# Channel mixing of the first batch spread over two attention batches, and four weight tiles converted ahead instead of twelve

## The chip, the cores and the metric

One core of a Trainium2 chip runs the whole program. The metric is the device time of one execution in microseconds (us). The engines named below are TensorE (PE, with its weight loads as PEld), VectorE (DVE), ScalarE (ACT), GpSimd (POOL) and SyncE (SP), whose queue issues nearly all DMAs.

## The reference

Three blocks follow each other on 4 batches of 448 tokens and 768 features, all in float32:

```python
attn_out = attn(q, k, v)                 # 12 heads of 64, causal mask, softmax
xt = x.transpose(0, 2, 1)                # x: attn_out as (batch, seq, 768)
h = relu(xt @ w_tok1) @ w_tok2           # token mixing, 448 -> 256 -> 448
u = x + h.transpose(0, 2, 1)
x = u + relu(u @ w_ch1) @ w_ch2          # channel mixing, 768 -> 1536 -> 768
theta = x @ w_theta
y = w_tok_r @ (x * cos(theta)) + w_tok_i @ (x * sin(theta))
u = x + y
out = u + relu(u @ w_ch)
```

The weights arrive as 64-bit floats. The chip rounds them to float32 and splits them into a high and a low part.

## The kernel before

**Attention.** Two heads make a pair, six pairs a batch, so there are 24 pairs. A pair has seven score tiles, and each tile is a *step*: 168 steps, 42 for a batch. `scores` (L252) does for one step the score matmul (L270), mask and row maximum on DVE (L277), the exponential on ACT (L279) and the transposition of the result. In pairs 0 to 11 PE transposes (L286) and ACT copies out (L288). From pair 12 (step 84) on, ACT and DVE split the result into two 16-bit halves (L107, L299) and a DMA transposes it (`pt<-ph`, L302), with three `ph` buffers. `pv` multiplies by the values four steps later, `finish` scales, and after every second pair `tokmix` does the token mixing for two 128-feature tiles of `u`. It also split each `u` tile into high and low parts (`ut`, nine buffers).

**Channel mixing** is cut into 96 *units*, 24 for a batch: 6 of `ch1_unit`, 6 of `ch2_unit`, and the same again for the second half of the 1536 features. A unit is 18 matmuls of 448 columns (L166 to L168, six tiles by three products) with one weight tile `ws` of 768 KB, and one evacuation on DVE (L387 or L395).

**Weights.** Each of the 24 channel weight tiles is converted once. ACT reads the raw data (L123), DVE does four bit operations (L130 to L134), ACT and DVE split it (L107, L114) into a `ws` tile (four buffers), and SP stores that to `w_c` (L433) for the later batches, which load it again (`ws<-w_c`, L161). `ROUND_STEPS` says at which step each conversion is written. Tiles below `EARLY` are converted ahead, stored, and loaded again when the first batch needs them. Tiles from `EARLY` on go from the conversion straight into their unit.

**Order.** Attention is written step by step with a priority of 500 instructions (`AHEAD`). Units and conversions are written between the steps without it, and a scheduler places them where it finds room, so they stand some steps behind the place where they are written. Once built, every engine and the SP queue run their own list strictly in its order. In the kernel before, unit number d*24//42 is written d steps after step 46: 24 units for each 42 steps.

**After attention** the remaining units run with the conversion of `w_theta` and `w_tok`, then the third block.

Of the kernel before, what the change touches and what calls it, by code (L numbers as in the profile page):

```python
# [19 lines left out]
B, H, S, D = 4, 12, 448, 64  # L20
E = H * D
NPR = H // 2
DT = E // P
# [5 lines left out]
BUFS = dict(ut=9, h2=6, acc=12, ws=4, wf=2, raw=2, sb=3, ph=3, pt=5)  # L29
NATIVE = {0, 1, 2, 3, 4, 5, 6, 7}  # L30
NATPV = {0, 1, 2, 3, 4, 5, 6, 7, 8, 9, 10, 11}
AHEAD, LAG, LOOK = 500, 4, 2
KEEP, UBACK = 6, 16
LATE_CONVERT = 16
EARLY = 12
ROUND_STEPS = [3, 4, 8, 9] + [19 + 3 * n for n in range(EARLY)] + [(169 + 7 * (n - 2)) // 4 + 2 for n in range(EARLY, 24)]
ENGINES = {
    0: dict(qhi="A", qlo="D", khi="A", klo="D", v="D", phi="A", xhi="A", xlo="D", uhi="A", ulo="D"),
}
# [10 lines left out]
def fused(ctx, tc, q, k, v, w_tok1, w_tok2, w_ch1, w_ch2, w_theta, w_tok, w_ch, out):  # L50
# [42 lines left out]
    def mm_bank():  # L93
        return bank("mm", 4)

    def hl_tile(tag):
        return main.tile([P, 2, S], F32R, tag=tag, name=tag, bufs=BUFS[tag])

    def acc_tile():
        return main.tile([P, S], F32, tag="acc", name="acc", bufs=BUFS["acc"])  # L100

    def f32v(ap):
        return ap.bitcast(F32)

    def copy_to(eng, dst, src, scale=1.0):
        if eng == "A":
            nc.scalar.activation(dst, src, AF.Copy, scale=scale)  # L107
        else:
            e = nc.gpsimd if eng == "P" else nc.vector
            e.tensor_scalar(out=dst, in0=src, scalar1=scale, scalar2=0.0, op0=ALU.mult, op1=ALU.add)  # L110

    def rest_to(eng, dst, src, hi):
        e = nc.gpsimd if eng == "P" else nc.vector
        e.tensor_tensor(out=dst, in0=src, in1=f32v(hi) if hi.dtype == F32R else hi, op=ALU.subtract)  # L114
# [24 lines left out]
    def split_w(dst, f):  # L139
        copy_to("A", dst[:, 0], f)  # L140
        rest_to("D", dst[:, 1], f, dst[:, 0])
# [6 lines left out]
    def ws_tile():  # L148
        return main.tile([P, 2, E], F32R, tag="ws", name="ws", bufs=BUFS["ws"])
# [9 lines left out]
    def stream_tile(kept):  # L159
        w = ws_tile()  # L160
        nc.sync.dma_start(out=f32v(w), in_=kept)  # L161
        return w

    def mm3(ps, a, b, ka, kb, first, last):

        nc.tensor.matmul(ps, lhsT=ka(a[:, 0]), rhs=kb(b[:, 0]), start=first, stop=False)  # L166
        nc.tensor.matmul(ps, lhsT=ka(a[:, 0]), rhs=kb(b[:, 1]), start=False, stop=False)  # L167
        nc.tensor.matmul(ps, lhsT=ka(a[:, 1]), rhs=kb(b[:, 0]), start=False, stop=last)  # L168
# [23 lines left out]
    def tok_weights(n):  # L192
        if n < 2:
            cols = slice(n * 512, (n + 1) * 512)
            return w_tok1[:, cols], wt1[:, :, cols]
        return w_tok2[:, (n - 2) * S:(n - 1) * S], wt2[:, n - 2]

    xbufs = []
# [142 lines left out]
        copy_to(pick("xhi"), xg[0][:, :, c], xb)  # L341
        rest_to(pick("xlo"), xg[1][:, :, c], xb, xg[0][:, :, c])

    def tokmix(g, xg, xb2, uT, acc):
        h1 = ap2.tile([P, 2, 2, TOK], F32R, tag="h1", name="h1", bufs=1)
        for t in range(2):
            ps = mm_bank()
            for i in range(4):
                wc = slice(i * TOK + t * P, i * TOK + (t + 1) * P)
                nc.tensor.matmul(ps[:, 0:TOK], lhsT=wt1[:, 0, wc], rhs=xg[0][:, i, :], start=(i == 0), stop=False)  # L350
                nc.tensor.matmul(ps[:, 0:TOK], lhsT=wt1[:, 0, wc], rhs=xg[1][:, i, :], start=False, stop=False)  # L351
                nc.tensor.matmul(ps[:, 0:TOK], lhsT=wt1[:, 1, wc], rhs=xg[0][:, i, :], start=False, stop=(i == 3))  # L352
            nc.scalar.activation(h1[:, t, 0, :], ps[:, 0:TOK], AF.Relu)
            nc.vector.scalar_tensor_tensor(out=h1[:, t, 1, :], in0=ps[:, 0:TOK], scalar=0.0, in1=f32v(h1[:, t, 0, :]),
                                           op0=ALU.max, op1=ALU.subtract)
        for pr2 in range(2):
            pst = mm_bank()
            xb = xb2[pr2]
            nc.tensor.matmul(pst[:, 0:64], lhsT=xb[:, 0, :], rhs=ident2, start=True, stop=True)
            for i in range(1, 4):  # L360
                nc.tensor.transpose(pst[:, 64 + P * (i - 1):64 + P * i], xb[:, i, :], ident)
            xt = acc_tile()
            nc.scalar.activation(xt, pst[:, 0:S], AF.Copy)
            ps = mm_bank()
            cut = slice(pr2 * P, (pr2 + 1) * P)
            for t in range(2):
                mm3(ps[:, 0:S], h1[:, t], wt2[:, t], lambda a: a[:, cut], lambda a: a, t == 0, t == 1)
            u = xt
            nc.vector.tensor_tensor(out=u, in0=ps[:, 0:S], in1=xt, op=ALU.add)
            acc[2 * g + pr2] = u  # L370
            t = hl_tile("ut")
            copy_to(pick("uhi"), t[:, 0], u)
            rest_to(pick("ulo"), t[:, 1], u, t[:, 0])
            uT[2 * g + pr2] = t


    h2 = {}
# [21 lines left out]
    uTs = [[None] * DT for _ in range(B)]  # L399
    accs = [[None] * DT for _ in range(B)]  # L400
    units = [(b, fh, c, t) for b in range(B) for fh in range(2) for c in (1, 2) for t in range(6)]
    loaded = {}
# [2 lines left out]
    late = [(w_ch[e], wd["c3", 0, e]) for e in range(DT)]  # L405

    def load_unit(n):
        if n < len(units) and n not in loaded:
            b, fh, c, t = units[n]
            loaded[n] = stream_tile(wd[f"c{c}", fh, t])  # L410

    fetched, rounding = {}, {}

    def fetch(j):
        if j < len(ROUND_STEPS):
            src = tok_weights(j)[0] if j < 4 else jobs[j - 4][0]
            fetched[j] = src, raw_tile()
            fetch64(*fetched[j])
# [6 lines left out]
    def round_rest(j):  # L425
        f = rounding.pop(j)
        round64(f, fetched.pop(j)[1])
        if j < 4:
            split_w(tok_weights(j)[1], f)
        else:  # L430
            w, kept = ws_tile(), jobs[j - 4][1]
            split_w(w, f)
            nc.sync.dma_start(out=kept, in_=f32v(w))  # L433
            if j - 4 >= EARLY:
                loaded[j - 4] = w
        fetch(j + 2)
# [3 lines left out]
    def convert_late(n):  # L440
        while made[0] < min(n, len(late)):
            with tc.issue_after(loads[min(LATE_CONVERT, max(loads))].ins):
                convert(*late[made[0]])
            made[0] += 1

    at = [0]

    def run_units(n):
        for _ in range(n):
            u = at[0]  # L450
            for ahead in range(LOOK + 1):
                load_unit(u + ahead)
            b, fh, c, t = units[u]
            if c == 1:
                ch1_unit(b, uTs[b], fh, t, loaded[u])
            else:
                ch2_unit(b, uTs[b], accs[b], fh, t, loaded[u])
            loaded[u] = None
            at[0] += 1


    eng, turn = dict(ENGINES[0]), {}

    def pick(what):
        turn[what] = turn.get(what, -1) + 1
        return eng[what][turn[what] % len(eng[what])]
# [3 lines left out]
    pairs, xgs = {}, {}  # L470

    def late_step(n):
        b, pr, t = steps[n]
        pp = pairs[b, pr]
        pv(pp, *TILES[t])
        if t == 6:
            if pr % 2 == 0:
                xgs[b, pr // 2] = [ap2.tile([P, 4, 2 * P], F32R, tag=f"xg{z}", name=f"xg{z}", bufs=1) for z in range(2)]
            finish(pp, xbufs[pr % 2], xgs[b, pr // 2])
            if pr % 2 == 1:  # L480
                tokmix(pr // 2, xgs[b, pr // 2], xbufs, uTs[b], accs[b])

    for n, (b, pr, t) in enumerate(steps):
        if t == 0:
            eng.update(ENGINES.get(b * NPR + pr, {}))
        if t == 0:
            pairs[b, pr] = Pair(b, pr, parts[b, pr])
        with tc.high_priority(AHEAD):
            scores(pairs[b, pr], *TILES[t])
        if n == 0:  # L490
            fetch(0)
            fetch(1)
        for j, at_step in enumerate(ROUND_STEPS):
            if at_step == n - 1:
                with tc.issue_after(pairs[b, pr].first.ins):
                    round_rest(j)
            if at_step == n:
                with tc.issue_after(pairs[b, pr].last.ins):
                    round_first(j)
        if n >= 140:  # L500
            convert_late((n - 136) // 4)
        if t == 0 and (b, pr) != (B - 1, NPR - 1):
            nx = (b + (pr + 1) // NPR, (pr + 1) % NPR)
            with tc.high_priority(AHEAD), ExitStack() as es:
                if nx == (0, 1):
                    es.enter_context(tc.issue_after(loads[0].ins))
                parts[nx] = prep(*nx)
        if n >= LAG:
            with tc.high_priority(AHEAD):
                late_step(n - LAG)  # L510
        done = n - LAG - 42
        if done >= 0:
            run_units(done * 24 // 42 + 1 - at[0])
    for n in range(len(steps) - LAG, len(steps)):
        late_step(n)
    convert_late(len(late))
# [110 lines left out]
    for b in range(B):  # L627
        raw, x2 = [], []
        for d in range(DT):
            r = acc_tile()  # L630
            nc.sync.dma_start(out=r, in_=x2d[b][d])
            t = hl_tile("ut")
# [126 lines left out]
```

## Time and profile before

| | |
|---|---|
| Median of 3 runs | 946.0 us (945.55 to 947.26) |
| Profiled execution, device time | 943.79 us |
| Its span, first to last instruction | 942.0 us |
| PE busy, PEld busy | 96%, 88% of the span |
| DVE, ACT, POOL busy | 67%, 41%, 12% |
| Mean granted clock of TensorE | 0.993 |
| Read from HBM, written to it | 150.14 MB, 34.60 MB |

Busy time counts an engine's instructions from start to end. Matmuls overlap each other, so a busy PE may still be waiting between two of them. A step is located in time by its score instruction on DVE (L277). The stretches used below end where steps 42, 51, 84, 112 and 161 begin: 86, 112.5, 240.9, 328.8 and 480.8 us, to within 0.3 us.

### The profile page before, as it was taken

The page shows a single profiled execution, that of the slowest core. Times are in us where ns is not written, and L with a number is a line of the kernel's source. Part 1 is how long each engine was busy: PE and PEld are TensorE (multiplying, and loading weights), DVE is VectorE, ACT ScalarE, POOL GpSimd, SP SyncE. Part 2 cuts the span into 40 slices and gives each one's busy share as a digit, 9 for nine tenths or more (in the row PEclk, how much of TensorE's full clock was granted, in tenths as well). Part 3 has the DMA queues.
Part 4 walks back from the last instruction along what each step waited for, and adds up shares of the span by engine and source line. Part 5 has one row for each costly group of instructions (what it writes and reads, how often), then busy time and mean ns, then how long its engine had stood idle before and what let it go on. Part 6 is the DMA issues. An engine that isn't in the chain of part 4 may idle for free.

```text
span 942.0 us, 15946 instructions
## 1 busy us (share of the span) xinstructions
PE 908.9 (96%) x5820; PEld 830.5 (88%) x5820; DVE 631.6 (67%) x1467; ACT 387.8 (41%) x914; POOL 109.3 (12%) x178
## 2 busy tenths in 40 slices
PE   7989799999999999998999999999999999999998
PEld 5878699999898888897989889989999999999997
DVE  5789765888977667856877268866675466485351
ACT  5777554667654546635535034332112202112100
POOL 2110000000000000000000000022531143242120
PEclk9999899999999999999999999999999999999999
DMA  5677997677879999999899879954604135153043
GB/s 167 200 226 252 353 343 255 236 250 267 262 222 317 271 274 208 235 271 225 229 269 311 274 256 380 313 195 150 217 1 150 40 130 148 46 159 98 33 130 126
DMA packets 104831, 199.96 MB, mean 212 GB/s; under 512 B 60912, under 2 KB 73008, under 8 KB 104752
## 3 DMA queue, kind: packets, MB, share of 16 engines
q1 hardware_dynamic: 103440, 197.13, 67.5%
q0 software_dynamic: 1152, 1.57, 0.8%
q8 instruction: 46, 0.75, 0.3%
q10 hardware_dynamic: 160, 0.23, 0.1%
q14 instruction: 33, 0.27, 0.1%
HBM read 150.14 MB, written 34.60 MB: 196 GB/s over the span
## 4 chain that ended last, share of the span: by engine, by line
PE 77%; DMA 11%; DVE 7%; ACT 2%; issue 2%; SPq 0%; POOL 0%; DVEq 0%; ACTq 0%; POOLq 0%
PE ps_mm L166 17%; PE ps_mm L167 17%; PE ps_mm L168 17%; DMA pt<-ph 6%; PE ps_pv L314 4%; PE ps_sc L270 3%; PE ps_sc L168 3%; PE ps_sc L166 3%; PE ps_sc L167 3%; DMA ws<-w_c 2%; PE ps_mm L286 2%; DMA raw<-in_w_ch_dram 1%; PE ps_pv L325 1%; PE ps_mm L351 1%; PE ps_mm L352 1%
## 5 line engine op out<-in xcount | busy, mean ns | idle before, releaser
L167 PE MATMUL ps_mm<-h,ws 128*128 128x448 f32 x432 | 159.1, 369 | 0.0
L166 PE MATMUL ps_mm<-h,ws 128*128 128x448 f32 x432 | 159.0, 369 | 0.0
L168 PE MATMUL ps_mm<-h,ws 128*128 128x448 f32 x432 | 158.9, 368 | 0.0
L166 PE MATMUL ps_mm<-ut,ws 128*128 128x448 f32 x288 | 107.3, 373 | 7.1 <-DMA ws<-w_c 7.1
L167 PE MATMUL ps_mm<-ut,ws 128*128 128x448 f32 x288 | 107.3, 373 | 0.0
L168 PE MATMUL ps_mm<-ut,ws 128*128 128x448 f32 x288 | 106.9, 371 | 0.0
L279 ACT ACTIVATE sb<-sb,mx 128x192 f32<-128x192 f32 (+3 forms) x168 | 89.6, 535 | 40.2 <-DVE mx L277 39.5
L166 PEld LDWEIGHTS ps_mm<-h,ws 128*128 128x128 f32 x432 | 81.2, 188 | 7.2 <-DMA ws<-w_c 0.2
L168 PEld LDWEIGHTS ps_mm<-h,ws 128*128 128x128 f32 x432 | 81.2, 188 | 7.0
L167 PEld LDWEIGHTS ps_mm<-h,ws 128*128 128x128 f32 x432 | 81.2, 188 | 6.9
L277 DVE CUSTOM_DVE_ANT_0 sb<-ps_sc,mask 128x192 f32<-128x192 f32 (+3 forms) x168 | 73.8, 455 | 12.5 <-PE ps_mm L286 10.3
L110 POOL TENSOR_SCALAR ut<-acc 128x448 fp32r<-128x448 f32 x24 | 16.9, 713 | 482.5 <-DMA acc<-x2d 472.6
L299 DVE SCALAR_TENSOR_TENSOR ph<-sb,ph 128x64 f16<-128x64 f32 (+3 forms) x156 | 42.8, 316 | 41.5 <-ACT ph L107 41.2
L563 ACT ACTIVATE tmp<-ps_sc 128x384 f32<-128x384 f32 x28 | 13.5, 483 | 132.2 <-PE ps_sc L168 132.1
L166 PEld LDWEIGHTS ps_mm<-ut,ws 128*128 128x128 f32 x288 | 54.7, 190 | 12.7 <-issue 5.1
L314 PE MATMUL ps_pv<-v_raw,ptf 128*128 128x128 f32 (+1 forms) x456 | 61.5, 276 | 3.1 <-ACT ptf L288 2.1
L314 PEld LDWEIGHTS ps_pv<-v_raw,ptf 128*128 128x128 f32 x456 | 57.4, 191 | 7.6 <-ACT ptf L288 3.9
L107 ACT ACTIVATE ph<-sb 128x192 f16<-128x192 f32 (+3 forms) x84 | 36.1, 443 | 60.3 <-DMA pt<-ph 59.8
L168 PEld LDWEIGHTS ps_mm<-ut,ws 128*128 128x128 f32 x288 | 54.7, 190 | 4.4 <-issue 0.2
L167 PEld LDWEIGHTS ps_mm<-ut,ws 128*128 128x128 f32 x288 | 54.7, 190 | 4.2
L395 DVE TENSOR_TENSOR acc<-ps_mm,acc 128x448 f32<-128x448 f32 x48 | 29.8, 620 | 34.6 <-PE ps_mm L168 34.5
L570 ACT ACTIVATE tmp<-tmp 128x384 f32<-128x384 f32 x28 | 14.7, 526 | 86.5 <-DVE tmp L568 86.5
(151 smaller groups left out, 2116.9 us busy)
## 6 DMA issues: line engine op xcount, KB each, us to landing
ws<-w_c SPq DMA_DIRECT2D x108, 768.0 KB, 5.8
raw<-in_w_ch_dram SPq DMA_DIRECT2D x30, 768.0 KB, 5.9
w_c<-ws SPq DMA_DIRECT2D x30, 768.0 KB, 4.8
q_raw<-in_q_dram SPq DMA_DIRECT2D x16, 448.0 KB, 5.1
k_raw<-in_k_dram SPq DMA_DIRECT2D x16, 448.0 KB, 6.4
v_raw<-in_v_dram SPq DMA_DIRECT2D x24, 288.0 KB, 4.2
x2d<-acc SPq DMA_DIRECT2D x24, 224.0 KB, 5.0
acc<-x2d SPq DMA_DIRECT2D x24, 224.0 KB, 3.8
```

The source lines that it names most:

```text
L107: nc.scalar.activation(dst, src, AF.Copy, scale=scale)
L110: e.tensor_scalar(out=dst, in0=src, scalar1=scale, scalar2=0.0, op0=ALU.mult, op1=ALU.add)
L166: nc.tensor.matmul(ps, lhsT=ka(a[:, 0]), rhs=kb(b[:, 0]), start=first, stop=False)
L167: nc.tensor.matmul(ps, lhsT=ka(a[:, 0]), rhs=kb(b[:, 1]), start=False, stop=False)
L168: nc.tensor.matmul(ps, lhsT=ka(a[:, 1]), rhs=kb(b[:, 0]), start=False, stop=last)
L270: nc.tensor.matmul(ps[:, 0:n], lhsT=lhs, rhs=cut(pp.kh), start=True, stop=pp.kl is None)
L277: pp.first = nc.vector.tensor_tensor_reduce(out=dst, in0=src, in1=msk, op0=ALU.add, op1=ALU.min, scale=-0.125, scalar=3.0e38, accum_out=pp ...
L279: pp.last = nc.scalar.activation(sb[:, 0:kk], sb[:, 0:kk], AF.Exp, bias=pp.mx[:, j:j + 1], scale=-1.0, accum_out=pp.sm[:, j:j + 1])
L286: nc.tensor.transpose(pst[:, u * P:(u + 1) * P], full[:, c0 + u * P:c0 + (u + 1) * P], ident)
L299: nc.vector.scalar_tensor_tensor(out=dst, in0=sb[:, c0:c1], scalar=PSC, in1=hi[:, c0:c1], op0=ALU.mult, op1=ALU.subtract)
L314: nc.tensor.matmul(pp.ps[:, reg:reg + n], lhsT=pt[:, u], rhs=pp.v[0][:, vt * D:vt * D + n], start=(u == 0), stop=(u == len(blks) - 1))
L395: nc.vector.tensor_tensor(out=acc[d], in0=ps[:, 0:S], in1=acc[d], op=ALU.add)
```

## The change

Three things change.

- **Units.** The list `UNIT_STEPS` replaces the even rate. Units 0 to 17 are written over steps 46 to 86, and from step 88 on the rate is 26 units for 42 steps, the first six of them the rest of batch 0. Before, all 24 units of batch 0 were written between steps 46 and 87.
- **Conversions.** `EARLY` is 4. Tiles 0 to 3 are converted at steps 20, 26, 32 and 38, and tile n from 4 on five steps before its unit, up to step 92. Before, tiles 0 to 11 were converted at steps 19 to 52, and the others up to step 81. So eight loads of `ws<-w_c` are gone. The first two loads are written at step 42.
- **Split of `u`.** `split_ready` makes the `ut` tiles when a `ut` buffer is known to be free, and no longer at once in `tokmix`.

```diff
-EARLY = 12
-ROUND_STEPS = [3, 4, 8, 9] + [19 + 3 * n for n in range(EARLY)] + [(169 + 7 * (n - 2)) // 4 + 2 for n in range(EARLY, 24)]
+FIRST_UNIT, PHASE, RATES = 46, 42, (18, 26)
+EARLY = 4
+UNIT_STEPS = [FIRST_UNIT + -(-n * PHASE // RATES[0]) if n < RATES[0] else
+              FIRST_UNIT + PHASE + -(-(n - RATES[0]) * PHASE // RATES[1]) for n in range(72)]
+ROUND_STEPS = [3, 4, 8, 9] + [20, 26, 32, 38] + [UNIT_STEPS[n] - 5 for n in range(EARLY, 24)]
...
     def load_unit(n):
-        if n < len(units) and n not in loaded:
+        if n < len(units) and n not in loaded and (n >= 24 or n in stored):
...
+    def split_ready():
+        while halves[0] < B * DT:
+            b, d = divmod(halves[0], DT)
+            if accs[b][d] is None or (d >= BUFS["ut"] - DT and at[0] < 24 * (b - 1) + 18):
+                return
+            t = hl_tile("ut")
+            copy_to(pick("uhi"), t[:, 0], accs[b][d])
+            rest_to(pick("ulo"), t[:, 1], accs[b][d], t[:, 0])
+            uTs[b][d] = t
+            halves[0] += 1
...
-        done = n - LAG - 42
-        if done >= 0:
-            run_units(done * 24 // 42 + 1 - at[0])
+        if n == FIRST_UNIT - 4:
+            load_unit(0)
+            load_unit(1)
+        run_units(sum(at_step == n for at_step in UNIT_STEPS))
```

Line numbers of the changed kernel are three higher up to `tokmix`: L280 is the score instruction that was L277, and L133 to L137 and L117 are the conversion. Further down, L394 is the unit's evacuation that was L395, and L445 the store that was L433.

On DVE at step 42 (the first row is its score; `wf` and `ws` rows are conversions), before:

```order
L277 ISA sb_148,mx<-ps_sc,mask_143 128x128
...
L133 SCALAR_TENSOR_TENSOR wf<-raw,wf 128x768
L130 TENSOR_SCALAR wf<-wf 128x768
...
L134 SCALAR_TENSOR_TENSOR wf<-raw,wf 128x768
L131 TENSOR_SCALAR wf<-wf 128x768
...
L277 ISA sb_148,mx<-ps_sc,mask 128x320
```

and now:

```order
L280 ISA sb_148,mx<-ps_sc,mask_143 128x128
L280 ISA mx 128x1
L137 SCALAR_TENSOR_TENSOR wf<-raw,wf 128x768
...
L117 TENSOR_TENSOR ws<-wf,ws 128x768
L280 ISA sb_148,mx<-ps_sc,mask 128x320
```

Two conversions stood interleaved here, and now one ends. Over DVE's list the conversion instructions (five a tile, or five for a piece of the token weights) change from 52 to 38 before the score of step 42, from 27 to 10 in steps 42 to 55 and from 55 to 58 in steps 56 to 83.

On DVE between the scores of steps 95 and 96 (320 and 448 columns, second pair of the part with 16-bit halves), before:

```order
L277 ISA sb_152,mx<-ps_sc,mask 128x320
...
L299 SCALAR_TENSOR_TENSOR ph<-sb_150,ph 128x64
L299 SCALAR_TENSOR_TENSOR ph<-sb_150,ph 128x256
L277 ISA sb_148,mx<-ps_sc,mask 128x448
```

and now:

```order
L280 ISA sb_152,mx<-ps_sc,mask 128x320
L280 ISA mx 128x1
L117 TENSOR_TENSOR v_mid<-v_raw 128x576
L335 TENSOR_TENSOR x_154<-ps_pv,sm 128x384
L340 TENSOR_SCALAR x_154<-ps_pv,sm 64x64 x2
L117 TENSOR_TENSOR ws<-wf,ws 128x768
L137 SCALAR_TENSOR_TENSOR wf<-raw,wf 128x768
L280 ISA sb_148,mx<-ps_sc,mask 128x448
```

Conversions now stand among the attention work of this part. In steps 84 to 111 DVE has 38 conversion instructions where it had 14, and in steps 112 to 125 four where it had none.

On the SP queue in the same part (`pt<-ph` is a transposing DMA of attention, `w_c<-ws` stores a converted tile, `raw` loads the next one), before:

```order
L302 DMA_TRANSPOSE pt<-ph 128x3x128
L302 DMA_TRANSPOSE pt<-ph 128x5x128
L161 DMA ws<-w_c_0_1_94 128x1536
L218 DMA q_raw<-in_q_dram 128x896
L220 DMA k_raw<-in_k_dram 128x896
L302 DMA_TRANSPOSE pt<-ph 128x5x128
```

and now:

```order
L305 DMA_TRANSPOSE pt<-ph 128x3x128 x2
L445 DMA w_c_1_1_112<-ws 128x1536
L123 DMA raw<-in_w_ch_dram 128x1536
L305 DMA_TRANSPOSE pt<-ph 128x5x128
L396 DMA x2d_0_69<-acc 128x448
L305 DMA_TRANSPOSE pt<-ph 128x5x128
```

A store and a load that wait for a conversion now stand between the transposing DMAs. On PE's list the unit matmuls, counted in units of 18, change from 2.1 to 2.1 in steps 42 to 55, from 15.9 to 11.9 in 56 to 83, from 13.8 to 10.0 in 84 to 111, from 24.4 to 29.2 in 112 to 160, and from 63.8 to 66.8 after that. One `tokmix` (two of the six tiles of a batch) moves from the third to the fourth of these parts.

## Rows read from the trace of the kernel before

**Rows 1.** The page's first part: PE's busy time and share of the span.

```profile
PE 908.9 (96%) x5820; PEld 830.5 (88%) x5820; DVE 631.6 (67%) x1467; ACT 387.8 (41%) x914; POOL 109.3 (12%) x178
```

**Rows 2.** Windows: stretch in us, its length, busy time of each engine.

```profile
core 0: us, PE busy (x) PEld busy (x) DVE busy (x) ACT busy (x) POOL busy (x), PEclk, DMA share, GB/s
0.00:86.00 86.00, 76.04 (x495) 64.57 (x496) 66.79 (x183) 61.24 (x162) 14.66 (x28) 0.98 0.67 208
86.00:112.50 26.50, 20.35 (x134) 17.46 (x133) 23.57 (x53) 17.71 (x42) 0.00 (x0) 0.95 0.88 309
112.50:240.90 128.40, 128.40 (x791) 120.10 (x790) 98.98 (x201) 75.80 (x167) 0.00 (x0) 0.98 0.75 270
240.90:328.80 87.90, 85.71 (x688) 77.14 (x687) 65.95 (x182) 49.71 (x121) 0.00 (x0) 1.00 0.95 276
328.80:480.80 152.00, 143.99 (x1243) 130.32 (x1240) 107.78 (x311) 78.99 (x200) 0.00 (x0) 1.00 0.93 237
480.80:942.00 461.20, 454.42 (x2484) 420.94 (x2482) 268.56 (x542) 104.36 (x225) 94.67 (x150) 1.00 0.53 171
75.00:100.00 25.00, 24.57 (x175) 21.53 (x174) 24.43 (x59) 21.12 (x55) 1.74 (x2) 0.99 0.80 276
850.00:900.00 50.00, 50.00 (x265) 46.87 (x263) 23.74 (x47) 11.61 (x24) 9.41 (x17) 1.00 0.25 82
```

**Rows 3.** Waits of PE, 86 to 112.5 us: total, times, longest.

```profile
PE ps_mm L166 <- DMA ws<-w_c: 4.8, 1, 4.8
```

**Rows 4.** Timeline of PE around unit 0: start us, us, instruction.

```profile
110.73 0.71 PE L166 MATMUL ps_mm<-ut,ws 128*128 128x448 f32 x1 [4.78 <-DMA ws<-w_c]
...
113.32 0.57 PE L168 MATMUL ps_mm<-ut,ws 128*128 128x448 f32 x1
...
116.31 0.54 PE L167 MATMUL ps_mm<-ut,ws 128*128 128x448 f32 x1
```

**Rows 5.** Timeline of PE in dense units: one matmul and the 18th after it.

```profile
616.12 0.37 PE L166 MATMUL ps_mm<-ut,ws 128*128 128x448 f32 x1
...
619.84 0.37 PE L166 MATMUL ps_mm<-ut,ws 128*128 128x448 f32 x1
```

**Rows 6.** Groups by line, forms apart: a conversion on DVE and ACT; a unit's evacuation.

```profile
L133 DVE SCALAR_TENSOR_TENSOR wf<-raw,wf 128x768 uint32<-128x768 uint32 x30 | 28.6, 954 | 0.3
L114 DVE TENSOR_TENSOR ws<-wf,ws 128x768 fp32r<-128x768 f32 x30 | 28.6, 953 | 4.9 <-ACT ws L107 4.5
L134 DVE SCALAR_TENSOR_TENSOR wf<-raw,wf 128x768 uint32<-128x768 uint32 x30 | 28.6, 952 | 0.2
L130 DVE TENSOR_SCALAR wf<-wf 128x768 f32<-128x768 f32 x30 | 16.7, 558 | 14.1 <-ACT wf L123 13.9
L131 DVE TENSOR_SCALAR wf<-wf 128x768 uint32<-128x768 uint32 x30 | 16.6, 554 | 0.3
L123 ACT ACTIVATE wf<-raw 128x768 f32<-128x768 f32 x30 | 27.3, 910 | 23.1 <-DMA raw<-in_w_ch_dram 14.1 <-DVE ws L114 5.1 <-DVE mx L277 1.8
L107 ACT ACTIVATE ws<-wf 128x768 fp32r<-128x768 f32 x30 | 25.1, 836 | 4.9 <-DMA w_c<-ws 2.6 <-PE ps_mm L168 1.7 <-DVE wf L134 0.5
L395 DVE TENSOR_TENSOR acc<-ps_mm,acc 128x448 f32<-128x448 f32 x48 | 29.8, 620 | 34.6 <-PE ps_mm L168 34.5
```

**Rows 7.** The chain that ended last, in order of time: start us, us, what.

```profile
38.75 0.12 PE ps_mm L351
...
41.57 0.20 PE ps_mm L167
```

**Rows 8.** Waits of the SP queue over the whole span.

```profile
SPq L120 <- DVE wf L134: 60.0, 23, 5.7
SPq L433 <- DVE ws L114: 37.8, 15, 8.8
```

**Rows 9.** Windows of PE alone: stretch in us, length, PE busy, granted clock.

```profile
72.50:75.50 3.00, 3.00 (x10) 0.50 0.78 231
111.00:116.50 5.50, 5.50 (x19) 0.50 1.00 390
```

More of the change, by code (lines that the diff above doesn't have):

```diff
@@ L342, in finish, with tokmix @@
         rest_to(pick("xlo"), xg[1][:, :, c], xb, xg[0][:, :, c])
-    def tokmix(g, xg, xb2, uT, acc):
+    def tokmix(g, xg, xb2, acc):
         h1 = ap2.tile([P, 2, 2, TOK], F32R, tag="h1", name="h1", bufs=1)
@@ L370, in tokmix @@
             acc[2 * g + pr2] = u
[L371 to L374, printed above, removed]
     h2 = {}
@@ L407, in load_unit @@
     def load_unit(n):
-        if n < len(units) and n not in loaded:
+        if n < len(units) and n not in loaded and (n >= 24 or n in stored):
             b, fh, c, t = units[n]
             loaded[n] = stream_tile(wd[f"c{c}", fh, t])
-    fetched, rounding = {}, {}
+    fetched, rounding, stored = {}, {}, set()
+    at, halves = [0], [0]
+    def split_ready():
[8 more added lines that the diff above has]
+            halves[0] += 1
     def fetch(j):
@@ L433, in round_rest @@
             nc.sync.dma_start(out=kept, in_=f32v(w))
+            stored.add(j - 4)
             if j - 4 >= EARLY:
@@ L444, in convert_late @@
             made[0] += 1
-    at = [0]
     def run_units(n):
@@ L459, in run_units @@
             at[0] += 1
+            split_ready()
     eng, turn = dict(ENGINES[0]), {}
@@ L480, in late_step @@
             if pr % 2 == 1:
-                tokmix(pr // 2, xgs[b, pr // 2], xbufs, uTs[b], accs[b])
+                tokmix(pr // 2, xgs[b, pr // 2], xbufs, accs[b])
+                split_ready()
     for n, (b, pr, t) in enumerate(steps):
```

## The prediction

> **What bounds the kernel now.** Read the busy line first: PE 96%, DVE 67%, ACT 41% [rows 1]. So PE looks like the bound, with 33 us idle. Matmuls overlap, so the weight loads are the better gauge. In a stretch of nothing but dense work they fill 46.87 of 50 us, 0.937 [rows 2]. Divide each stretch's PEld time by 0.937, and you have the time that PE needs there. What is left is its slack:
>
> - 0 to 86 us (steps 0 to 41, attention of batch 0): needs 68.9, slack 17.1
> - 86 to 112.5 (steps 42 to 50): needs 18.6, slack 7.9
> - 112.5 to 240.9 (steps 51 to 83): needs 128.2, slack 0.2
> - 240.9 to 328.8 (steps 84 to 111): needs 82.3, slack 5.6
> - 328.8 to 480.8 (steps 112 to 160): needs 139.1, slack 12.9
> - 480.8 to the end: needs 449.2, slack 12.0
>
> That is 56 us in all, 25 of it before the first unit runs. (The Trainium skill, "Perfetto Trace Analysis", section Identifying the Most-Contended Engine, says that matmul occupancy is no good measure and points to the weight loads; here it is 96% against 88% [rows 1], and by the first the change could save 33 us at most.)
>
> Now look for what holds PE up where it has slack. From 86 to 112.5 us DVE is busy 23.57 of 26.5 us, 0.89, and from 75 to 100 us 24.43 of 25, 0.98 [rows 2]. There DVE is the bound. At the end of this stretch PE waits 4.8 us for a reloaded weight tile [rows 3], and then runs at half clock, 1.2 GHz, from 111 to 116.5 us [rows 9]. Matmuls start 0.374 us apart there (2.99 us for eight [rows 4]), where they start 0.207 apart in dense work. From 112.5 to 240.9 us PE is the bound, and DVE still reaches 0.77 [rows 2].
>
> **The change part by part.** The work is the same in sum, less eight reloads on DMA, so the question is where PE's slack goes. Two prices. A unit costs PE 18 starts in 3.72 us [rows 5] and DVE 0.62. A conversion costs DVE 0.954 + 0.953 + 0.952 + 0.558 + 0.554 = 3.97 us and ACT 0.910 + 0.836 = 1.75 us [rows 6]. The counts per stretch stand with the order rows of the change.
>
> *Steps 0 to 41.* DVE loses 14 conversion instructions, 2.8 tiles, 11 us of 66.8. PE's slack there is 17.1 us, but the first steps, with the start and the token weights, don't change, and PE, ACT and DVE hand work round in a ring. Bounds: nothing, if the ring sets the pace, and 8, if DVE does alone. I take half, -4.
>
> *Steps 42 to 50.* Four conversions shrink to about one, so DVE falls from 23.6 to some 12 us, and the reload is written at step 42, so the wait of 4.8 us goes. PE, with 18.6, is late next. At most -7.9, and at least the wait, -4.8. I take -7, since nothing else was late.
>
> *Steps 51 to 83.* PE loses 4.0 units, 14.9 us, and the half clock at the start (5.5 us at 0.374 instead of 0.207 a start, 2.5 us) should go with the wait. DVE keeps its 99 us: half a conversion more, four evacuations less. That is 0.89 of the 111 us that are left to PE, just what DVE reached from 86 to 112.5. So I give back 1.4: -16. Bounds -17.4 and -9 (DVE at 0.83).
>
> *Steps 84 to 111.* This is the heart of it. PE loses 3.8 units, 14.1 us, and one token mixing: 24 starts of 0.12 and 12 of 0.20 us [rows 7] and some transposes, 6 us. So PE needs 62 us. DVE gains 24 conversion instructions, 4.8 tiles or 19.1 us, and loses four evacuations (2.5) and the token mixing's share (about 2): 66.0 + 19.1 - 4.5 = 80.5 us. DVE is now 18 us longer than PE, and is the bound. The tiles that PE needs next come out of the same queue just before, so PE cannot fill its time with them. At the share of 0.977, DVE's best over 25 us, the stretch takes 82.4 us; at 0.89, the share when PE depended on it, 90.4. I take 87, so -1, with 82.4 and 94 (6 us over the top, for waits on SP) as ends. PE's slack rises from 5.6 to 25 us.
>
> *Steps 112 to 160.* PE gains 4.8 units, 17.9 us, and the token mixing, 6: 23.9. More units leave less of the 12.9 us slack open; I take 3 of it back. +21, bounds 18 and 24.
>
> *From step 161.* Three units more, +11 (11.2, all dense work), bounds 9 and 12.
>
> *Cost nothing:* the eight reloads less, 6 MB, run beside PE work, but for the one that PE waited for, counted above. The later split of `ut` is the same DVE and ACT work. If its cover went, a late `ut` would hold a unit for one DVE and one ACT instruction of 448 columns, about 0.6 us each like the evacuation [rows 6], which is under the bounds above.
>
> Sum: -4 - 7 - 16 - 1 + 21 + 11 = +4 us. Span 942.0 + 4 = 946; the profiled execution took 943.79, and its kernel's median is 946.0, 2.2 above, so I state it on the median: **950.0 us**. In words: the early slack is emptied, and about as much, and a little more, opens again in steps 84 to 111.
>
> **The rivals.**
>
> *DVE closes up: faster.* In steps 84 to 111 DVE runs at 0.977 (82.4 us, -5.5), and the early gains come in full: -6, -7.9, -17.4, and then +19 and +11. That is -6.8, 939. For it: DVE did run so for 25 us [rows 2], and its instructions there depend little on PE. Against: those 25 us held native attention, without the wait on transposing DMAs. The point from which it decides is 84 us or so for that stretch. Chance 0.30, with all that is faster.
>
> *Gains and losses cancel.* A microsecond or two less in steps 84 to 111 or in the start: 946. Chance 0.18.
>
> *The SP queue blocks attention.* In steps 84 to 111 five more pairs of store and raw load stand before transposing DMAs. SP waited for a conversion 2.5 us a store and 2.6 us a load (37.8 us for 15, 60.0 for 23 [rows 8]). Five times 5.1 is 26 us. With half of it behind DVE work that is late anyway, the time is +12 more, 962. For it: a blocked transposition keeps one of three `ph` buffers. Against: the queue's order follows DVE's, so SP mostly waits for what DVE is about to do. Chance 0.12.
>
> *PE's clock falls again.* PE ran at half clock from 72.5 to 75.5 and from 111 to 116.5 us [rows 9], each time after it had waited, the second time after 4.78 us [rows 4]. With 25 us of slack in steps 84 to 111, three such drops, at 2.5 us each, would give +7.5, 957. Against: PE has its slack there in small pieces, and in a stretch that DVE bounds a slower PE costs little. Chance 0.08. (The Trainium skill, "TensorE: Matmul & The Clock Gate", section Part 1: The HAM clock gate, says that the throttled state is the default and that activity releases it, so a rule that speaks against thinning PE's work out; both rows agree with it.)
>
> **How the numbers follow.** A difference of 0.2%, 1.9 us, is about what a measurement of this kernel can tell from none. My forecast of a small loss has 0.32, the SP queue 0.12 and the clock 0.08: slower 0.52. Within the bound 0.18. Faster 0.30. The likeliest case by itself spans 947 to 956. The range for eight in ten reaches down to the full gain of the first rival and a little under it, and up to the SP case: 937 to 962.
>
> **What would show it.** Right: step 42 begins at about 82 us, unit 0 starts before 100 us with no wait of 4.8 us and no half clock. Step 84 begins at some 214 us; steps 84 to 111 take 85 us or more with DVE above 0.88 and PEld near 58 us, and PE waits at L169 for a `ws` tile's conversion (L117, or ACT's L110). The last stretch is 11 us longer. Wrong: if PEld in steps 84 to 111 fills over 0.75 of the stretch, it is faster than I say. If the start gains under 8 us, attention's own ring, and not the conversions, set its pace, and the loss is larger. If PE waits there for `pt<-ph`, the SP case holds.

## The result and the profile after

The change is faster: 937.49 us median against 945.55, a ratio of 0.9909 with a 95% interval of 0.9881 to 0.9936. I had forecast 950.0, slower. It came out near the first rival's time (939), though not quite by its way. Timed again beside other kernels, the ratio was 0.9915 (0.9889 to 0.9941).

The busy line of the profile after, where [rows 1] stood before:

```profile
PE 903.5 (97%) x5820; PEld 827.0 (89%) x5820; DVE 633.0 (68%) x1467; ACT 389.5 (42%) x914; POOL 109.5 (12%) x178
```

The span is 933.7 us, 8.3 less than before. The windows below are cut where steps 42, 51, 84, 112 and 161 begin in the kernel after, with the columns of [rows 2], whose first six rows are the same stretches before:

```profile
0.00:81.10 81.10, 74.25 (x499) 63.54 (x500) 58.31 (x170) 57.07 (x157) 14.94 (x28) 1.00 0.58 174
81.10:102.40 21.30, 21.30 (x147) 19.10 (x146) 11.61 (x35) 12.38 (x33) 0.00 (x0) 1.00 0.76 263
102.40:210.30 107.90, 105.99 (x682) 98.26 (x681) 95.53 (x200) 74.47 (x165) 0.00 (x0) 1.00 0.72 250
210.30:290.50 80.20, 66.86 (x559) 59.27 (x558) 76.71 (x195) 50.71 (x118) 0.00 (x0) 0.98 0.93 260
290.50:461.80 171.30, 170.89 (x1411) 156.69 (x1409) 120.13 (x333) 89.34 (x217) 0.00 (x0) 1.00 0.92 265
461.80:933.70 471.90, 464.26 (x2533) 430.12 (x2531) 270.69 (x542) 105.51 (x225) 94.54 (x150) 1.00 0.53 171
```

With PE's need and slack reckoned as in the prediction:

| Steps | Length before, after | Forecast, measured change | Slack forecast, measured |
|---|---|---|---|
| 0 to 41 | 86.0, 81.1 | -4, -4.9 | 13.1, 13.3 |
| 42 to 50 | 26.5, 21.3 | -7, -5.2 | 0.9, 0.9 |
| 51 to 83 | 128.4, 107.9 | -16, -20.5 | 1.6, 3.0 |
| 84 to 111 | 87.9, 80.2 | -1, -7.7 | 25, 16.9 |
| 112 to 160 | 152.0, 171.3 | +21, +19.3 | 9.9, 4.1 |
| 161 to the end | 461.2, 471.9 | +11, +10.7 | 12, 12.9 |
| Sum | 942.0, 933.7 | +4, -8.3 | 62, 51 |

The start, the late steps and the end came as forecast, to within 2 us each. Steps 51 to 83 and 84 to 111 came out shorter than forecast, by 4.5 and 6.7 us. In steps 84 to 111 PE did run dry, as the prediction said, but less, and the steps behind them closed up more. DVE held that stretch. From 245 to 280 us it was busy for 34.83 of 35 us, and PE's weight loads filled 22.09:

```profile
245.00:280.00 35.00, 26.00 (x242) 22.09 (x240) 34.83 (x88) 20.81 (x48) 0.00 (x0) 0.95 1.03 292
```

What PE waited for in steps 84 to 111 (total, times, longest):

```profile
PE ps_pv L328 <- DMA pt<-ph: 8.6, 6, 2.1
PE ps_mm L169 <- DMA ws<-w_c: 1.7, 1, 1.7
PE ps_pv L328 <- issue: 1.2, 1, 1.2
PE ps_mm L171 <- DVE ws L117: 1.0, 3, 0.4
PE ps_mm L169 <- ACT ws L110: 0.5, 1, 0.5
```

Most of it is for attention's transposing DMAs, and 1.5 us for conversions, where the prediction had expected the conversions to show. That left open whether DVE or the SP queue made the transpositions late.

### The profile page after: what moved, and what is told of

Its sections match the earlier page's. It is cut to its first block, busy times and chain, and to the rows that moved or that the text cites. A ratio compares the mean times of both kernels' runs of the same rounds, so it can differ in the third digit from the quotient of the medians.

```text
span 933.7 us, 15879 instructions
## 1 busy us (share of the span) xinstructions
PE 903.5 (97%) x5820; PEld 827.0 (89%) x5820; DVE 633.0 (68%) x1467; ACT 389.5 (42%) x914; POOL 109.5 (12%) x178
## 4 chain that ended last, share of the span: by engine, by line
PE 75%; DMA 12%; DVE 8%; ACT 3%; issue 2%; POOL 0%; SPq 0%; ACTq 0%; POOLq 0%; DVEq 0%
PE ps_mm L169 17%; PE ps_mm L170 17%; PE ps_mm L171 17%; DMA pt<-ph 7%; PE ps_sc L273 3%; PE ps_pv L317 3%; PE ps_sc L170 3%; PE ps_sc L169 3%; PE ps_sc L171 3%; PE ps_pv L328 2%; DMA ws<-w_c 2%; PE ps_mm L289 2%; DMA raw<-in_w_ch_dram 1%; DMA q_raw<-in_q_dram 1%; PE ps_sc L275 1%
## 5 line engine op out<-in xcount | busy, mean ns | idle before, releaser
L280 DVE CUSTOM_DVE_ANT_0 sb<-ps_sc,mask 128x192 f32<-128x192 f32 (+3 forms) x168 | 74.6, 454 | 15.2 <-PE ps_mm L289 11.1
L577 ACT ACTIVATE tmp<-ps_sc 128x384 f32<-128x384 f32 x28 | 13.5, 483 | 132.2 <-PE ps_sc L171 132.1
L302 DVE SCALAR_TENSOR_TENSOR ph<-sb,ph 128x64 f16<-128x64 f32 (+3 forms) x156 | 42.9, 316 | 27.3 <-ACT ph L110 26.7
L386 DVE SCALAR_TENSOR_TENSOR h<-ps_mm,h 128x448 fp32r<-128x448 f32 x48 | 29.7, 618 | 34.2 <-ACT h L385 34.0
```

The costliest lines, as they stand in the source:

```text
L280: pp.first = nc.vector.tensor_tensor_reduce(out=dst, in0=src, in1=msk, op0=ALU.add, op1=ALU.min, scale=-0.125, scalar=3.0e38, accum_out=pp ...
L302: nc.vector.scalar_tensor_tensor(out=dst, in0=sb[:, c0:c1], scalar=PSC, in1=hi[:, c0:c1], op0=ALU.mult, op1=ALU.subtract)
L386: gates[0] = nc.vector.scalar_tensor_tensor(out=t[:, 1], in0=ps[:, 0:S], scalar=0.0, in1=f32v(t[:, 0]), op0=ALU.max, op1=ALU.subtract)
```

## The experiments

My theory was that the change is two changes: relief of DVE at the start, which gains, and a spread of units and conversions, which costs. The rivals were that the spread makes the gain, or the eight reloads that are gone. The later split of `u` is in all kernels below that start from the change, and none tests it by itself.

**The halves apart.** The first kernel has the new conversions with the old even rate of units. The second has the new rate with the old twelve tiles ahead:

```diff
-FIRST_UNIT, PHASE, RATES = 46, 42, (18, 26)
+FIRST_UNIT, PHASE, RATES = 46, 42, (24, 24)
```

> The change with the old even rate of units (24 for 42 steps in every batch), so only the conversions move: four ahead, the others five steps before their unit. DVE has 38 and 5 conversion instructions before steps 42 and 51 (the change 38 and 2, before 52 and 18), but 90 in steps 51 to 83 (66, 64) and 15 in 84 to 111 (38, 14). Theory A, the gain is the start, and conversions in steps 84 to 111 only cost: step 51 at about 102 us, and in steps 51 to 83 DVE needs 99 + 26 x 0.79 = 120 us where PE needs 128, so PE stays the bound there: 930 to 934 us of span, as fast as the change or faster. Theory B, the spread of the units makes the gain (slack of steps 112 to 160 fell from 12.9 to 4 us): 938 to 943. Theory C, the eight reloads less make it: 934, as the change, since these are gone here too.

```diff
-EARLY = 4
-ROUND_STEPS = [3, 4, 8, 9] + [20, 26, 32, 38] + [UNIT_STEPS[n] - 5 for n in range(EARLY, 24)]
+EARLY = 12
+ROUND_STEPS = [3, 4, 8, 9] + [19 + 3 * n for n in range(EARLY)] + [UNIT_STEPS[n] - 5 for n in range(EARLY, 24)]
```

> The change with twelve tiles converted ahead at the old steps and loaded again, so the units' rate alone is new (and the first two loads written at step 42). Conversion instructions on DVE: 52 and 17 before steps 42 and 51, as before the change; 38 in steps 84 to 111, as in the change. Theory A (the start makes the gain): step 51 at 107 to 112 us, steps 84 to 111 in about 80 us as in the change, 938 to 943. Theory B (the spread makes it): 933 to 936. Theory C (the reloads make it): 940 to 943.

Measured: the even rate with four ahead has 0.9845 (0.9809 to 0.9882), span 925.5. The spread alone has 0.9997 (0.9975 to 1.002), span 944.1. The second kernel also has the first two loads at step 42, which gain a little by themselves (next experiment), so the spread costs somewhat more than the 0.9997 shows. Its steps 42 to 50 and 84 to 111:

```profile
84.70:109.90 25.20, 22.35 (x139) 19.18 (x137) 22.00 (x52) 15.67 (x39) 0.00 (x0) 0.93 0.89 326
215.90:299.10 83.20, 70.98 (x562) 63.45 (x561) 75.86 (x194) 50.95 (x120) 0.00 (x0) 0.90 0.94 259
```

So the gain comes with four tiles ahead instead of twelve, and not with the spread. Step 51 begins at 112.8 us in the kernel before and at 109.9 in the spread alone, but between 101.6 and 104.5 in every kernel that converts four tiles at steps 20 to 38. The missing reloads don't make this part: by step 51 three have been issued in the kernel before and four in the change. Behind step 51 the eight reloads and the conversions changed together, and no run parts them. The windows of the even rate, cut at the same steps:

```profile
0.00:80.90 80.90, 74.30 (x499) 63.63 (x500) 58.26 (x169) 57.03 (x157) 14.94 (x28) 1.00 0.58 174
80.90:103.30 22.40, 21.90 (x150) 19.68 (x149) 13.42 (x40) 13.54 (x35) 0.00 (x0) 1.00 0.75 261
103.30:229.10 125.80, 123.05 (x766) 113.70 (x765) 115.61 (x230) 84.27 (x178) 0.00 (x0) 1.00 0.79 279
229.10:312.70 83.60, 80.77 (x657) 73.57 (x657) 65.56 (x182) 48.85 (x120) 0.00 (x0) 1.00 0.94 269
312.70:470.20 157.50, 151.65 (x1322) 137.85 (x1321) 113.49 (x322) 79.68 (x201) 0.00 (x0) 1.00 0.93 249
470.20:925.50 455.30, 448.97 (x2435) 416.21 (x2433) 266.30 (x534) 104.20 (x223) 93.74 (x150) 1.00 0.53 169
```

Step 51 begins at 103.3 us, 0.9 later than in the change. In the third row DVE is busy 0.92 of the stretch, and PE has 4.5 us of slack there (7.4 in a second profiled execution of this kernel), where it had 0.2 before. This execution was the fastest of its five; the ratio is the safer figure.

**The reload that PE waited for**, in the kernel before:

```diff
+        if n == 42:
+            load_unit(0)
+            load_unit(1)
         done = n - LAG - 42
```

> The kernel before, with its first two weight reloads written at step 42 instead of beside unit 0. Theory A1, PE's wait of 4.8 us and the half clock behind it (2.5 us) are half of the gain of the start: -5 to -7, 935 to 937 of span. Theory A2, DVE's conversions hold the start up and the wait only shows what is late last there: 0 to -2.

Measured: 0.9963 (0.994 to 0.9986), some 3.5 us by the median ratio, between what the two theories gave. The one profiled execution, 944.9 us of span, was the slowest of twelve, so its rows show what holds the stretch and not the gain:

```profile
86.10:111.40 25.30, 22.23 (x138) 18.92 (x137) 21.87 (x52) 15.68 (x39) 0.00 (x0) 0.93 0.90 328
```

In it PE waits for no reload, and steps 42 to 50 still take 25.3 us, with DVE at 0.86 and the clock still falling. The spread alone, with these loads and the old conversions, takes 25.2 us there, and the change, with the new conversions, 21.3. So the wait was mostly what came last, and the conversions set that stretch.

**The stores on another queue**, in the change:

```diff
-            nc.sync.dma_start(out=kept, in_=f32v(w))
+            (nc.gpsimd if j - 4 >= EARLY else nc.sync).dma_start(out=kept, in_=f32v(w))
```

> The change with the stores of the converted tiles from 4 on issued by GpSimd's queue instead of SP's, so that they no longer stand before transposing DMAs. PE waited 8.6 us for those transpositions in steps 84 to 111 of the change. If the SP queue holds them up: -3 to -6, 928 to 931 of span. If DVE is what they are late from: 933 to 935, no change.

Measured: 0.989 (0.9857 to 0.9922), span 932.6, not to be told from the change. PE still waited 5.4 us for `pt<-ph` in that stretch (the change 8.6), and DVE was busy 79.84 of 85.1 us. So the stores in the SP queue cost no time that shows, though some of that wait may be theirs. In the change the SP queue itself waits there most of all before transposing DMAs, and only 5.4 us for a conversion's store (waits of SP, 210 to 290 us):

```profile
SPq L305 <- DVE ph L302: 10.2, 9, 2.7
SPq L305 <- ACT h L356: 7.4, 3, 5.3
SPq L445 <- DVE ws L117: 5.4, 3, 3.7
```

The raw loads stayed on SP, so for these nothing is shown.

**Less DVE work in the conversions of the last eight tiles**, in the change; the kernel leaves out three of the four bit operations for these:

```diff
         nc.vector.tensor_scalar(out=f, in0=f, scalar1=W64_MIN, scalar2=None, op0=ALU.max)
+        if light:
+            return
...
-        round64(f, fetched.pop(j)[1])
+        round64(f, fetched.pop(j)[1], j - 4 >= 16)
```

> The change, with the three integer operations on DVE (shift and the two merges, 2.46 us a tile) left out of the conversion of the last eight weight tiles, 16 to 23, so those weights are wrong. 20 us of DVE work go from steps 82 to 100. Conversion instructions in steps 84 to 111: 21, the change 38; the scheduler then places 15.3 units there instead of 9.9. Theory A (DVE's conversions cost PE its slack of 17 us in steps 84 to 111): that slack falls to about 5 us, as before the change, and the span to 921 to 925. Theory B (attention's transposing DMAs, for which PE waited 8.6 us there, are what holds it up): the slack stays over 12 us, 930 to 934.

Measured: 0.9869 (0.9835 to 0.9903), span 934.1. Half of theory A held. The two rows are steps 84 to 111 and 112 to 160:

```profile
210.20:308.20 98.00, 95.90 (x732) 87.56 (x730) 74.47 (x198) 57.81 (x134) 0.00 (x0) 0.98 1.00 301
308.20:462.10 153.90, 146.44 (x1250) 131.06 (x1248) 108.64 (x309) 79.82 (x200) 0.00 (x0) 0.99 0.91 237
```

Slack in the first fell to 98.0 - 87.56/0.937 = 4.6 us, as forecast. The scheduler also placed 15.3 units there instead of 9.9, so the conversions open that slack directly or by keeping units out; this run does not tell the two apart. In the second stretch slack rose to 14.0, from 4.1 in the change, with 23.9 units there instead of 29.2. The span did not move, and the ratio moved by no more than its interval. This was the find: the slack of one stretch is given back by the other.

**The rate in steps 112 to 160.** So the number of units in these steps should set their slack. In the change, with the early part kept:

```diff
-FIRST_UNIT, PHASE, RATES = 46, 42, (18, 26)
+FIRST_UNIT, PHASE, RATES = 46, 42, (18, 22)
```

> The change (18 and 26, 933.7 us of span) with a rate of 22 after the first 42 steps, so that 24.7 units stand in steps 112 to 160 instead of 29.2, and the early steps with their conversions stay. Theory A (units fill attention's gaps there): slack in 112 to 160 back to 12 to 14 us from 4.1, 941 to 943 of span, which is what the prediction's sum had come to. Theory B: 933 to 935.

Measured: 1.0024 (1.0002 to 1.0045), median 947.06, span 942.2. The rows of steps 84 to 111 and 112 to 160:

```profile
210.20:289.90 79.70, 67.08 (x568) 59.66 (x567) 77.11 (x196) 50.96 (x119) 0.00 (x0) 0.98 0.94 261
289.90:454.10 164.20, 159.00 (x1320) 143.25 (x1320) 119.94 (x334) 86.42 (x217) 0.00 (x0) 0.99 0.93 265
```

The first stretch is as in the change (slack 16.0). In the second, slack is back at 11.3 from 4.1. With 27.3 us of slack in the two stretches this kernel comes nearest to my sum, which had 35, and so does its median. The rate of 26 against 22 is worth 1.1 to 1.2% here, some 10 us.

The same the other way, from the even rate. First lower, 22 after the first 42 steps (`RATES` (24, 22)):

> The even rate with four tiles ahead (925.5 us of span), then 22 units for 42 steps from step 88 on instead of 24: 23.4 units in steps 112 to 160 (25.3). Theory A (units fill attention's gaps there, at about 1.6 us each, also without the conversions in steps 84 to 111): slack 12 to 14 us there from 10.4, 928 to 929 of span. Theory B (they do so only behind the stretch that DVE holds up): 925 to 926.

Measured: 0.992 (0.9889 to 0.9951), span 938.2, against 0.9849 for the even rate beside it. The row of steps 112 to 160:

```profile
323.00:469.50 146.50, 140.73 (x1203) 125.49 (x1202) 106.16 (x308) 79.80 (x204) 0.00 (x0) 1.00 0.96 247
```

That is theory A's direction, with 12.6 us of slack, but the loss, 0.7% or 7 us, is larger than the 2.5 to 3.5 us that it gave. Then higher, with batch 2's units 1.4 and 1.25 steps apart:

```diff
+UNIT_STEPS[48:] = [130 + -(-(n - 48) * 7 // 5) for n in range(48, 72)]
```

> The even rate with four tiles ahead (925.5 us of span), with the 24 units of batch 2 written 1.4 steps apart from step 130 on, not 1.75. The list has 27.4 units in steps 112 to 160 (25.3). Theory A (a unit more in these steps fills about 1.6 us that attention leaves PE idle: over the kernels so far 24.4 units went with 13 us of slack, 29.2 with 4 to 6): slack 7 us there (10.4), 922 of span. Theory B (the slack only moves behind step 161, where fewer units are left beside the last steps): 925.

> As e11_late14 with units 1.25 steps apart, 28.4 units in steps 112 to 160. Theory A: slack 5 to 6 us there, 920 to 921 of span. Theory B: 925 or above, with slack after step 161 over the 11.1 us of the even rate.

Measured: 0.9877 (0.9855 to 0.99), span 930.7, and 0.9902 (0.9872 to 0.9931), span 930.5. Theory A failed here. The last two rows of the second kernel:

```profile
315.50:480.20 164.70, 159.96 (x1330) 146.16 (x1329) 113.59 (x319) 79.08 (x199) 0.00 (x0) 0.99 0.89 246
480.20:930.50 450.30, 443.25 (x2427) 410.42 (x2425) 266.51 (x536) 105.06 (x225) 94.39 (x150) 1.00 0.52 168
```

Slack in steps 112 to 160 fell to 8.7 us only, from 10.4, and the end kept 12.3. That is what theory B forecast, but the even rate has 12.1 at the end in a second execution, so it says little for B's reason. Crowding the last batch on top of the even rate gains nothing, for a reason that no run shows.

**The conversions at their even places, the units spread**, so that all 24 tiles are stored and loaded again:

```diff
-EARLY = 4
+EARLY = 24
-... [UNIT_STEPS[n] - 5 for n in range(EARLY, 24)]
+... [41 - (-n * 7 // 4) for n in range(4, 24)]
```

> The change's units (18 and 26), but the conversions from tile 4 on at the steps that fit the even rate, five before the old place of their units, up to step 82, and all 24 tiles stored and loaded again. So the spread of the units stands without the conversions in steps 84 to 111 (26 instructions, the change 38, the even rate 15), and 20 more reloads run. Theory A (conversions in steps 84 to 111 are the cost of the spread): slack there 5 to 10 us, 925 to 929 of span. Theory B (fewer units there, so nothing to fill PE with, is the cost): 933 to 935. If the reloads cost: above 935, with PE waiting for ws<-w_c.

Measured: 1.0022 (1.0001 to 1.0044), span 944.4. Up to step 51 it is as early as the even rate (103.4 us), with every tile stored for a reload. Behind it the reloads cost, and the question it was made for stays undecided. Two rows of PE's waits from 103 to 321 us:

```profile
PE ps_mm L169 <- DMA ws<-w_c: 15.2, 3, 8.9
PE ps_sc L273 <- DVE mx L280: 1.7, 1, 1.7
```

**In between, and further.** The rates (21, 25), and two tiles ahead at the even rate (`EARLY = 2`, steps 26 and 36):

> The change with 21 units over the first 42 steps and 25 for 42 after (the change 18 and 26, even rate 24 and 24). Conversion instructions in steps 51 to 83: 82 (66 and 90), in 84 to 111: 25 (38 and 15). Theory A (the price of the spread is what DVE has to do in steps 84 to 111 over what PE needs there): between the two but nearer the even rate, since 25 instructions put DVE at about 72 us where PE needs 80: 925 to 928 of span. Rival (the price grows with each unit that is moved): half way, 929 to 930.

> The even rate with four tiles ahead (925.5 us of span), but two tiles converted ahead instead of four, at steps 26 and 36. Conversion instructions: 29 before step 42 (38), 15 in steps 42 to 50 (5), 89 in 51 to 83 (90). Theory A (the start gains as long as DVE holds it up): DVE share up to step 42 was 0.72 with four ahead, so it holds up no more there, and 15 instructions in 42 to 50 come back: -1 to +3, 925 to 929. Rival (every tile less ahead is worth 1.3 us, as eight tiles less were worth 10): -3, 922 to 923.

Measured: 0.9868 (0.9835 to 0.9901), span 932.3, and 0.9884 (0.9852 to 0.9917), span 930.7. The first lies between the change and the even rate; its span lies above both theories, and its interval tells neither from the other. In the second, step 42 begins 2.5 us earlier, at 78.4, but steps 42 to 50 take 27.9 us instead of 22.4: their DVE work rises from 13.42 to 22.16 us. That is theory A's way, and a little worse than its range. Four ahead is enough, and two is no better.

```profile
0.00:78.40 78.40, 71.58 (x483) 61.61 (x484) 50.97 (x158) 53.40 (x151) 14.55 (x28) 1.00 0.48 136
78.40:106.30 27.90, 25.26 (x171) 22.76 (x170) 22.16 (x52) 19.35 (x46) 0.00 (x0) 1.00 0.85 295
```

**The change and the even rate side by side.**

> The change itself, next to the even rate with four tiles ahead, on one chip and against the same runs of the kernel before. If spreading the units costs (933.7 us of span against 925.5 so far): ratio to before 0.989 to 0.993. If the two spans differed by chance: both ratios within 0.3% of each other.

> The even rate with four tiles ahead once more, beside the change. If spreading the units costs 6 us: ratio to before 0.983 to 0.987, lower than the change's by 0.4% or more. By chance: 0.988 to 0.991.

Measured: 0.9915 (0.9889 to 0.9941) for the change and 0.9849 (0.9822 to 0.9876) for the even rate with four tiles ahead. The spread does cost, 0.66% or 6 us. The even rate is the best kernel of the study: 932.28 us against 946.07 for the kernel before beside it. Steps 84 to 111 and 112 to 160, of the change and then of the even rate:

```profile
210.00:290.80 80.80, 68.87 (x563) 61.41 (x562) 76.81 (x195) 50.76 (x118) 0.00 (x0) 0.96 0.94 262
290.80:461.60 170.80, 170.11 (x1406) 155.99 (x1405) 120.21 (x333) 88.86 (x217) 0.00 (x0) 1.00 0.91 264
232.40:314.90 82.50, 80.14 (x653) 72.77 (x653) 64.96 (x181) 48.96 (x120) 0.00 (x0) 1.00 0.96 272
314.90:474.00 159.10, 153.73 (x1322) 139.47 (x1322) 113.42 (x322) 79.89 (x201) 0.00 (x0) 0.99 0.93 246
```

Slack is 15.3 and 4.3 us in the change, 4.8 and 10.3 in the even rate. A second execution of the same kernel gave the slack of steps 112 to 160 again to within 0.2 us, and that of steps 84 to 111 to within 1.7.

## Why the prediction was wrong

**Right: the start.** Steps 0 to 50 were to give 11 us and gave 10.1; the half clock was to go and went (granted clock 1.00 in both rows, 0.98 and 0.95 in [rows 2]). The reason given, DVE's early conversions, is confirmed by when step 51 begins: at 109.9 to 112.8 us in the kernels with twelve tiles ahead, at 101.6 to 104.5 in those with four by step 42.

**Right: DVE becomes the bound in steps 84 to 111, and the spread costs.** DVE was busy 0.956 of that stretch, and with less of its work, and more units, the slack there closed (4.6 us). Side by side, the spread costs 6 us.

**Wrong: the size of that cost.** By the prediction's own terms the start and the half clock were -13.5, so the rest of the change was +17.5 us. It was measured at +6. The steps that failed are terms of the sum, two of them for slack:

- *"At 0.89, the share when PE depended on it, 90.4. I take 87."* The stretch took 80.2 us, below the end that I had given, 82.4, and PE's slack was 16.9 and not 25. About 4 us of the difference are DVE's work: 76.7 us and not 80.5. I had added the durations of single instructions, and their recorded times overlap. Those of all DVE instructions that start in the stretch add up to 77.3 us before and 91.0 after, near the rise of 14.5 that I forecast, while the busy time rose by 10.7 only. The rest, some 3 us, is the share: 0.956, and 0.995 in 35 us of it, where I took 0.925. The 0.89 came from a stretch that ended in a wait for a reload [rows 3], but with that wait gone the share there was still 0.86; what kept DVE from more is not shown.
- *"More units leave less of the 12.9 us slack open; I take 3 of it back."* 8.8 us came back. Units fill the slack of steps 112 to 160: in this order of the conversions, 24.7 units left 11.3 us and 29.2 left 4.1, an estimate of 1.6 us for each unit. I had a count of units for that stretch and no price for what one fills.
- *"PE loses 4.0 units, 14.9 us"*, in steps 51 to 83, which gave 20.5 us and not 16. By its weight loads PE needed 23.3 us less there, not 17.4, and 28.1 more in steps 112 to 160, not 23.9. The counts were taken on PE's list between its scores, from step 56 on, and the stretches are cut by DVE's scores from step 51 on, so work stood in another stretch than I thought. This moved time between stretches and little of the sum.

Over steps 84 to 111 and 112 to 160 I forecast 35 us of slack, and 21 was measured. These 14 us are the miss of 12.3, within 2 us. The pattern over the kernels, with units counted on PE's list:

| Kernel | Units in 112 to 160 | Slack in 84 to 111 | Slack in 112 to 160 | Sum |
|---|---|---|---|---|
| before | 24.4 | 5.6 | 12.9 | 18.5 |
| the change | 29.2 | 16.9 | 4.1 | 21.0 |
| light conversions | 23.9 | 4.6 | 14.0 | 18.6 |
| rate 22 after 18 | 24.7 | 16.0 | 11.3 | 27.3 |
| even rate, four ahead | 25.3 | 5.1 | 10.4 | 15.5 |
| rates 21 and 25 | 24.4 | 6.5 | 14.5 | 21.0 |
| spread alone | 29.2 | 15.5 | 5.5 | 21.0 |
| units 1.25 steps apart | 28.4 | 5.8 | 8.7 | 14.5 |

In the other kernels, too, 23.4 to 24.5 units went with 10.6 to 13.7 us of slack in steps 112 to 160, 27.4 with 8.5, and 29.2 with 4.3 to 6.2. So more units go with less slack there, but at no single price: from the even rate's 25.3 units to 28.4 it is half a microsecond each. In these kernels a stretch that is short of units keeps its gaps, and moving units from one to another moves much of the gaps with them. The prediction treated steps 84 to 111 by themselves, found that they would run dry, and missed that the units not run there would be worth something later.

**The rivals.** The first one's place and point were right: DVE closed up, and the stretch fell below 84 us. Its time, 939, is near by a smaller gain in steps 0 to 50 (10.1 us, not 13.9) and a larger one in steps 51 to 111 (28.2, not 22.9). The SP queue's chance is not borne out: with its stores moved away the time stayed within the interval. Its sign did show, PE's waits for `pt<-ph` (8.6 us), so that sign could not tell it from a late DVE. The sign for "faster", PEld over 0.75 of the stretch, did not show (0.74), though the stretch was faster. The clock fell in steps 84 to 111, where its mean is 0.98; a short window shows the drop:

```profile
261.00:271.00 10.00, 7.68 (x37) 6.10 (x37) 9.89 (x23) 6.37 (x14) 0.00 (x0) 0.83 0.93 267
```

A mean of 0.98 over 80.2 us makes about 3 us at half clock, one drop's worth and not three. In the second execution of the change the mean is 0.96, two drops' worth, and the span 1.5 us longer.

**Open:** why units crowded into the last batch on top of the even rate fill so little, why two units fewer there cost more than the slack that they leave, how much of the even rate's gain behind step 51 is the eight reloads, and what the later split of `u` does.

## What to carry to other kernels

When a change moves filler work between stretches, price the filler at both ends: what runs dry where it leaves, and which gaps it fills where it goes. Here the first was seen and the second was sized by feel. A share of an engine from one stretch is no ceiling for another, durations added up are not busy time, and a change made of two edits is best read as two, since here one half gave 14 us and the other took 6 back.

(The Trainium skill, "Perfetto Trace Analysis", section Optimization Strategy, says that where the most-contended engine changes over time, interleaving the regimes may help. The trace agrees for the start, where the conversion instructions of six tiles, 70 of DVE's against 40 now, left a stretch that DVE bound. The spread shows the limit: steps 84 to 111, where most of them went, changed hands from PE to DVE.)

## What the hardware showed that I had not expected

- DVE was kept busy for 34.83 of 35 us by a queue of short instructions in steps where PE, ACT and transposing DMAs all take part. I had not thought over 0.98 possible with those dependencies.
- The recorded times of DVE's instructions overlap: over the kernel before they add up to 717 us, and DVE is busy for 632.
- PE fell to half clock after short waits only: from 210 to 290 us it waited 2.1 us at the longest, and the granted clock over 261 to 271 us had a mean of 0.83.
